# Attention followed by a soft mixture of experts: slot sums from the accumulated D^T P, grouped narrow products, and an output in larger chunks

## The chip, the cores and the metric

The kernel runs on one core of one Trainium2 chip. The metric is the device time of one execution in microseconds (us). The engines are called as the profile calls them: PE (TensorE; PEld is its weight load), DVE (VectorE), ACT (ScalarE), POOL (GpSimd) and SP (SyncE, which here only issues DMAs).

## The reference, cut to what matters

```python
kv_pool = kv.reshape(B, H//4, 4, W//4, 4, C).mean(axis=(2, 4))
k = v = kv_pool.reshape(B, -1, C) @ w_sr               # 768 keys per batch, C = 128
a = softmax((q @ k.T) / sqrt(C), -1);  x = (a @ v).reshape(B * S, D)   # B = 4, S = 12288 queries
logits = x @ phi                                       # 49152 tokens x 32 slots
d = exp(logits - logits.max(0)); d /= d.sum(0) + 1e-9  # softmax over the tokens
slot_input = d.T @ x                                   # 32 x 128
slot_out = per expert e (8, of 4 slots): relu(slot_input @ w1[e]) @ w2[e]   # hidden 1024
c = exp(logits - logits.max(1)); c /= c.sum(1) + 1e-9  # softmax over the slots
out = c @ slot_out                                     # 49152 x 128
```

Inputs and output are float32. `q` is given to the kernel transposed, and the output is written transposed (`outT`, 128 x 49152).

## The kernel before

The kernel never forms x. With P the unnormalised attention weights of a tile, logits are (P U)/rowsum with U = v phi (768 x 32), and the slot input is (D^T P) v.

**A tile** is 128 queries; there are 384, 96 in each batch. `qk` (L348) makes scores in one of three score slots in PSUM (`sslot`, tag "s", two banks each) from high and low parts of q and k, six matmuls. `top` (L358) finds the row maximum on DVE, `exp` (L365) makes P in float32 on ACT with its row sum, `hi` and `lo` (L377 on ACT, L381 on POOL) split the first 512 of 768 keys into two float16 halves, and `turn` (L384) turns these by DMA transposes issued on SP. The last 256 keys are turned in PE for two tiles at a time (`tp`, L389) and copied out by DVE (`tev`, L396).

**A group** is eight tiles; the last eight form two groups of four, which makes 49 groups. `lmm` (L405) makes its logits, transposed, in the bank "L": `lmm(g, 0)` from the float32 part, then three more steps from the float16 parts. Their weights are 32 columns wide and four of them share the PE array side by side. `lt_out`, `lt_turn`, `recip`, `logits` scale and turn them back into `LL`, which keeps the logits of all tokens. `colmax`, `cross`, `newmax` update the running column maximum, `weights` makes e = exp(logits - max) on ACT, and `scaled` divides by the row sums, which gives D. `total_mm` (L516) sums e over the tokens by matmuls against a vector of ones, and `total` (L525) adds this to the running sum `EA`, faded by `decay` when the maximum has moved. `ymm` (L532) makes D^T P of two tiles, in four steps y0, y2, y4, y6, in the bank "D"; its weights too are 32 columns wide. `yacc` adds it to `acc`. `rowmax`, `rowsub` (POOL), `rowexp` turn `LL` into the unnormalised c.

**A batch** begins with its keys (loaded by SP, added up by POOL in eight steps during the batch before: `kv_load`, `kv_add`, `kv_fold`) and ends with `yturn` and `slots`, which multiply acc with v and add to the slot input `SA`.

**The bank D** is shared: the turned tiles of `tp`, D^T P and the key products use it one after the other (ring "D" of one). The bank L has a ring of one as well.

**The order on every engine** is made ahead by a planner (`Plan`, L26): each operation has an engine, a cost, a latency, dependencies, buffers that it takes and a priority; the planner runs through time and always lets an engine take the operation of smallest priority among those that can start within 0.12 us of the first one. `LATE` shifts the priorities by kind of operation.

**The tail** first loads the expert weights (4 MB each of w1 and w2) into buffers that the tiles leave, then runs the experts (`t_sm` to `t_slo`). `k_sum`, `k_add`, `k_rec`, `k_mul` (L882 to L897) make the row sums of c for 16 tiles at a time, add eps, take the reciprocal and multiply (POOL). The output goes by chunks of CH = 3 quads (a quad is four tiles): `c_t` turns c in PE, `c_hi` and `c_lo` split it, `o_mm` (L916) multiplies it with the slot outputs, 32 rows at a time, into two score slots, `o_ev` copies one on DVE and the other on ACT into one buffer, and `o_dma` (L936) writes it. The first two chunks are written by halves (two of each four tiles), all others whole.

Of the kernel before, what the change touches and what calls it, by code (L numbers as in the profile page):

```python
# [19 lines left out]
P = 128  # L20
# [5 lines left out]
class Plan:  # L26
# [3 lines left out]
    HOLD = 0.7  # L30
# [6 lines left out]
    def op(self, eng, cost, lat, prio, deps, fn, acq=(), use=(), at=0.0, raw=0.1, hot=False):  # L37
        n = len(self.ops)
        for key in list(acq) + list(use):
            self.users.setdefault(key, []).append(n)  # L40
        self.ops.append((eng, cost, lat, prio, [d for d in deps if d is not None], fn, list(acq), at, raw, hot, list(use)))
        return n

    def emit(self):
# [18 lines left out]
        free = dict.fromkeys(avail, 0.0)  # L63
        todo = len(ops)
# [10 lines left out]
        def best(e):  # L75
            found = []
            for n in avail[e]:
                t = acquire(n)
                if t is not None:
                    found.append((max(free[e], ready[n], t), ops[n][3], n))  # L80
            if not found:
                return None
            t0 = min(found)[0] + 0.12
            hot = [f for f in found if ops[f[2]][9]]
            if hot:
                h = min(hot)
                if h[0] - t0 < self.HOLD:
                    fits = [(p, t, n) for t, p, n in found if t <= t0 and t + ops[n][1] <= h[0] + 0.1]
                    return min(fits) if fits else (h[1], h[0], h[2])
            return min((p, t, n) for t, p, n in found if t <= t0)  # L90

        self.starts = [None] * len(ops)
        while todo:
# [7 lines left out]
            self.starts[n] = t  # L101
            free[e] = t + cost
# [20 lines left out]
def attention_then_soft_moe(ctx: ExitStack, tc: tile.TileContext, qT, kv0, kvT, w_sr, w_srT, phi, w1, w2, outT):  # L123
# [59 lines left out]
    eps = cp.tile([P, 1], F32, tag="eps", name="eps")  # L183
    nc.vector.memset(eps, EPS)
# [14 lines left out]
    EA = cp.tile([P, 1], F32, tag="EA", name="EA")  # L199
    MB = cp.tile([P, NS], F32, tag="MB", name="MB")  # L200
# [204 lines left out]
    def lmm(g, n):  # L405
# [3 lines left out]
        if n == 0:  # L409
            G[g] = {"L": bank("L", f"L_{g}")}  # L410
# [105 lines left out]
    def total_mm(g):  # L516
        G[g]["D"] = bank("D", f"D_{g}")
        n = groups[g][1] // NQD
        for x in range(n):
            nc.tensor.matmul(  # L520
                G[g]["D"][:, NT * NS : NT * NS + 1], G[g]["e"][:, x * NQD : (x + 1) * NQD, :], ones[:, :1],
                start=(x == 0), stop=(x == n - 1),
            )

    def total(g):  # L525
        t = G[g]["D"][:, NT * NS : NT * NS + 1]
        if g:
            nc.vector.scalar_tensor_tensor(out=EA, in0=EA, scalar=G[g]["al"], in1=t, op0=ALU.mult, op1=ALU.add)
# [29 lines left out]
    def rowexp(g):  # L558
        nc.scalar.activation(ll(g), ll(g), AF.Exp, scale=-1.0)

# [34 lines left out]
    def pool(n):  # L595
# [85 lines left out]
    def group_ops(g):  # L681
# [4 lines left out]
        lk = ("L", g)  # L686
# [15 lines left out]
        l0 = (0.52 if n == GMAX else 0.3, 0.2)  # L702
        l1 = (0.44 if n == GMAX else 0.3, 0.2)
        a = go("l0", "PE", l0, [ops["tev", u] for u in us] + [ops["u", b]], lambda: lmm(g, 0), acq=[lk], use=pfs + [("U", b)])
        for x in range(3):
            a = go(f"l{x + 1}", "PE", l1, [a] + (turns if x == 0 else []), lambda x=x: lmm(g, x + 1), use=[lk, ("U", b)] + pts, raw=0.0)
# [5 lines left out]
        a = go("cx", "PE", (0.24, 0.25), [a], lambda: cross(g), use=[lk])  # L712
# [4 lines left out]
        al = go("al", "ACT", (0.19, 0.1), [a], lambda: decay(g)) if g else None  # L717
        d = go("dp", "DVE", dv(0.33), [w, rc], lambda: scaled(g), acq=[("dp", g)], use=[lk, ("e", g)])
        y = t = go("tm", "PE", (0.22 * n / GMAX, 0.25), [w], lambda: total_mm(g), acq=[("D", g)], use=[("e", g)])
        for t0 in range(0, n, 2):  # L720
            y = go(f"y{t0}", "PE", (0.67, 0.2), [y, d], lambda t0=t0: ymm(g, t0, t0 + 2), use=[("dp", g), p32[t0 // 2], ("D", g)], raw=0.0)
        ya = go("ya", "DVE", (0.42, 0.08), [y, al, ops.get(("yt", b - 1)) if first else ops["ya", g - 1]], lambda: yacc(g), use=[("D", g)])
        go("to", "DVE", (0.13, 0.08), [y, al, ops.get(("to", g - 1))], lambda: total(g), use=[("D", g)])
        rm = go("rm", "DVE", dv(0.33), [sb], lambda: rowmax(g))
        rm = go("rs", "POOL", dv(0.57, 0.02), [rm], lambda: rowsub(g))
        ops["c", g] = go("re", "ACT", dv(0.31, 0.1), [rm], lambda: rowexp(g))
        if (s + n) % TPB == 0:
# [3 lines left out]
            ops["sl", b] = sl  # L731
            m = go("ms", "DVE", (0.35, 0.1), [ops["nm", g], ops.get(("sa", b - 1))], lambda: mstep(b, g), use=[lk])
# [5 lines left out]
    for i in range(NTL):  # L738
        b = i // TPB
        t = T(i)  # L740
        iq = i // TB
        if i % TB == 0:
            if iq >= 1 and iq + 2 < NB:
                ops["q", iq + 2] = op("SP", 0.75, 2.0, t - 2, [ops["ql", iq - 1], ops["q", iq + 1]], lambda n=iq + 2: q_load(n), acq=[("q", iq + 2)])
            for n in ([0, 1] if iq == 0 else [iq + 1]):
                if n < NB:
                    a = op("ACT", 0.54, 0.1, t + LATE["qh"] if n else -50, [ops["q", n], ops.get(("ql", n - 1))], lambda n=n: q_hi(n), acq=[("qs", n)], use=[("q", n)])
                    ops["ql", n] = op("POOL", 1.24, 0.02, t + LATE["ql"] if n else -50, [a], lambda n=n: q_lo(n), use=[("qs", n), ("q", n)])
        kd = [ops["k", b, 0], ops["k", b, 1]]
        ops["qk", i] = op("PE", 1.03, 0.24, t + LATE["qk"], [ops["ql", iq], ops.get(("qk", i - 1))] + kd, lambda i=i: qk(i), acq=[("s", i)], use=[("qs", iq), ("kT", b)], raw=0.0)  # L750
        a = op("DVE", 0.92, 0.06, t + LATE["top"], [ops["qk", i]], lambda i=i: top(i), use=[("s", i)])
        ops["e", i] = op("ACT", 0.89, 0.1, t + LATE["exp"], [a, ops.get(("e", i - 1))], lambda i=i: exp(i), acq=[("p32", i // 2)] if i % 2 == 0 else [],
                         use=[("s", i)] + ([("p32", i // 2)] if i % 2 else []), raw=0.0)
        a = ops["hi", i] = op("ACT", 0.53, 0.1, t + LATE["hi"], [ops["e", i], ops.get(("hi", i - 1))], lambda i=i: hi(i), acq=[("hl", i)], use=[("p32", i // 2)], raw=0.15)
        a = op("POOL", 1.12, 0.02, t + LATE["lo"], [a], lambda i=i: lo(i), use=[("hl", i), ("p32", i // 2)])
        ops["turn", i] = op("SP", 1.45, 2.2, t + 6, [a, ops.get(("turn", i - 1))], lambda i=i: turn(i), acq=[("pt", i // 2)] if i % 2 == 0 else [],
                            use=[("hl", i)] + ([("pt", i // 2)] if i % 2 else []))
        if i % 2:
            u = i // 2
            dk = ("D", ("t", u))  # L760
            a = op("PE", 0.38, 0.24, t + LATE["tp"], [ops["e", i]], lambda u=u: tp(u), acq=[dk], use=[("p32", u)], raw=0.0)
            ops["tev", u] = op("DVE", 0.6, 0.06, t + LATE["tev"], [a, ops.get(("tev", u - 1))], lambda u=u: tev(u), acq=[("pf", u)], use=[dk])
# [20 lines left out]
    CH = 3  # L783
# [98 lines left out]
    def k_sum(x):  # L882
        o, n = kg[x]
        nc.vector.tensor_reduce(out=RM[:, o : o + n], in_=LL[:, o : o + n, :], axis=X, op=ALU.add)

    def k_add(x):
        o, n = kg[x]
        nc.scalar.activation(RM[:, o : o + n], RM[:, o : o + n], AF.Identity, bias=eps)

    def k_rec(x):  # L890
        o, n = kg[x]
        nc.vector.reciprocal(out=RM[:, o : o + n], in_=RM[:, o : o + n])  # L892

# [12 lines left out]
    def c_hi(g):  # L906
        n = chunks[g][1] * P
        UC[g, "c"] = ring("pt", [P, 2, HK], F32R, f"c_{g}")
# [18 lines left out]
    def o_ev(g, u):  # L927
        n = chunks[g][1] * P
        src = UC[g, "po", u][:, :, :n].rearrange("p t (j q) -> p t j q", q=P)
        dst = UC[g, "o"][:, :, 2 * u : 2 * u + 2, :].rearrange("p j t q -> p t j q")  # L930
# [5 lines left out]
    def o_dma(g, t0, t1):  # L936
        o, n = chunks[g]
        nc.sync.dma_start(
            out=outT[:, o * TS * P : (o + n) * TS * P].rearrange("p (j t q) -> p j t q", t=TS, q=P)[:, :, t0:t1, :],
            in_=UC[g, "o"][:, :, t0:t1, :],  # L940
# [21 lines left out]
    a = tail("PE", 0.3, [ops["to", LAST]], t_es, acq=[("L", "pe")])  # L962
# [27 lines left out]
    for x, (o, n) in enumerate(kg):  # L990
        w = n * NS
        p = T1 + 288 + 4 * x
        need = [ops["c", GOF[o]], ops["c", GOF[o + n - 1]]]
        a = op("DVE", dve(w), 0.08, p, need + [qt if x < 6 else slo], lambda x=x: k_sum(x))
        a = op("ACT", 0.18, 0.08, p, [a], lambda x=x: k_add(x))
# [60 lines left out]
```

## Time and profile before

| what | us |
|---|---|
| runs | 987.91, 987.96, 994.11; median 987.96 |
| the profiled execution's own time | 990.42 |
| its span | 988.6 |
| mean granted PE clock in it | 0.956 |
| busy: PE, DVE, ACT, POOL | 916.7, 758.2, 745.2, 693.3 |

The page says how long each engine was busy, how the 40 slices of the span look, and which groups of instructions cost most. Answers of the trace show single instructions in order of time (start and length in us from the span's start), the busy time of each engine in a stretch, and the chain of waits that ended last. "L537" is line 537 of the kernel before. The planner repeats the same order for many groups, so one group read instruction by instruction says much about the loop. fp32 matmuls are recorded as two instructions.

### The profile page before, as it was taken

What the parts mean: (1) busy time and instruction counts of PE and PEld (TensorE: products, weight loads), DVE (VectorE), ACT (ScalarE), POOL (GpSimd) and SP (SyncE); (2) the same over time, 40 slices, a digit from 0 to 9 for tenths busy, and PEclk for the clock granted to TensorE, in tenths of its full rate; (3) what the DMA queues carried; (4) which work ended last, traced back from release to release, by engine and by line L of the source; (5) the groups of instructions that cost most, each with busy time, mean ns of one, the idle gap of its engine ahead of it and who ended that gap; (6) DMA issues with size and microseconds to landing.
All of it is one profiled execution on the core that took longest, in us unless ns stands there. A gap on an engine that the chain in (4) does not pass through costs nothing.

```text
span 988.6 us, 27483 instructions
## 1 busy us (share of the span) xinstructions
PE 916.7 (93%) x10392; PEld 773.8 (78%) x10392; DVE 758.2 (77%) x1894; ACT 745.2 (75%) x1571; POOL 693.3 (70%) x584
## 2 busy tenths in 40 slices
PE   0999999999999999999999999999999999968875
PEld 0878988888888888888888888888798989844543
DVE  6667888788768787877778788788687888846775
ACT  1688888888868887878868888888688888813554
POOL 2498999876779988876789989767577777612222
PEclk9999999999999999999999999999999999987566
DMA  7499999897889999987999999988698898992877
GB/s 303 91 233 181 203 210 212 156 161 139 157 212 199 205 189 182 163 152 151 163 226 204 189 204 171 170 139 153 127 155 162 155 163 149 127 349 75 337 302 324
DMA packets 433011, 186.49 MB, mean 189 GB/s; under 512 B 408560, under 2 KB 410352, under 8 KB 432880
## 3 DMA queue, kind: packets, MB, share of 16 engines
q1 hardware_dynamic: 432304, 184.35, 87.9%
q8 instruction: 81, 1.33, 0.5%
q10 hardware_dynamic: 576, 0.41, 0.1%
q14 instruction: 50, 0.41, 0.1%
HBM read 58.87 MB, written 25.17 MB: 85 GB/s over the span
## 4 chain that ended last, share of the span: by engine, by line
PE 47%; DVE 4%; ACT 3%; issue 1%; DMA 0%; DVEq 0%; ACTq 0%; SPq 0%
PE s L356 20%; PE DB L537 8%; PE L L414 6%; PE DB L394 4%; PE po L925 3%; DVE o L934 1%; PE DB L520 1%; PE L L439 1%; ACT hl L379 1%; DVE junk L360 1%; ACT p L372 1%; ACT o L932 1%; PE ph L826 1%; PE DB L904 1%; DVE pf L398 0%
## 5 line engine op out<-in xcount | busy, mean ns | idle before, releaser
L382 POOL TENSOR_TENSOR hl<-p,hl 128x512 f16<-128x512 f32 x384 | 442.2, 1167 | 144.1 <-ACT hl L379 128.2
L356 PE MATMUL s<-kT,qs 128*128 128x384 f32 x2304 | 479.5, 350 | 2.3 <-ACT p L372 2.3
L360 DVE CUSTOM_DVE_ANT_1 junk<-s,lnpk 128x768 bf16<-128x768 f32 x384 | 366.2, 954 | 70.8 <-PE s L356 52.5
L356 PEld LDWEIGHTS s<-kT,qs 128*128 128x128 f32 x2304 | 392.4, 190 | 25.1 <-issue 19.1
L372 ACT ACTIVATE p<-s,nm 128x768 f32<-128x768 f32 x384 | 344.7, 899 | 89.1 <-PE DB L537 41.7
L379 ACT ACTIVATE hl<-p 128x512 f16<-128x512 f32 x384 | 235.2, 625 | 5.5 <-DMA pt<-hl 0.7
L346 POOL TENSOR_TENSOR qs<-q,qs 128x512 fp32r<-128x512 f32 x96 | 125.2, 1304 | 45.9 <-ACT qs L343 27.9
L398 DVE COPY pf<-DB 128x512 f32<-128x512 f32 x192 | 131.8, 686 | 19.4 <-PE DB L394 12.8
L537 PE MATMUL DB<-p,dp 128*32 128x192 f32 x3072 | 146.7, 332 | 0.0
L394 PE MATMUL DB<-ident,p 128*128 128x128 f32 x768 | 118.4, 276 | 12.1 <-DVE pf L398 9.1
L537 PEld LDWEIGHTS DB<-p,dp 128*32 128x32 f32 x3072 | 90.5, 110 | 29.2 <-issue 9.2
L394 PEld LDWEIGHTS DB<-ident,p 128*128 128x128 f32 x768 | 95.0, 141 | 22.0 <-DVE pf L398 10.2
L255 POOL TENSOR_TENSOR LL<-LL 128x1536 f32<-128x1536 f32 x21 | 73.3, 3491 | 2.6 <-DMA LL<-kvT 2.3
L372 ACT ACTIVATION_READ_ACCUMULATOR p<-s,nm 128x1 f32 x384 | 74.7, 195 | 0.0
L414 PE MATMUL L<-pt,u 128*32 128x256 f16 (+1 forms) x2352 | 73.5, 272 | 0.0
L897 POOL TENSOR_TENSOR LL<-LL,RM 128x512 f32<-128x512 f32 x24 | 24.9, 1048 | 67.1 <-DVE RM L892 67.1
L414 PEld LDWEIGHTS <-u 128*32 128x32 f16 x2352 | 63.9, 98 | 10.0 <-issue 1.9
L343 ACT ACTIVATE qs<-q 128x512 fp32r<-128x512 f32 x96 | 59.8, 623 | 11.8 <-DMA q<-qT 9.6
L414 PE MATMUL L<-pf,us 128*32 128x256 f32 (+1 forms) x784 | 54.1, 394 | 0.0
L925 PE MATMUL po<-c,shl 32*128 32x384 f32 x384 | 40.4, 502 | 13.8 <-DVE o L934 11.2
L435 ACT ACTIVATE lt<-L,g 128x256 f32<-128x256 f32 (+1 forms) x49 | 23.0, 469 | 38.7 <-PE L L414 38.7
L932 ACT ACTIVATE o<-po 128x768 f32<-128x768 f32 x32 | 25.9, 810 | 29.0 <-PE po L925 29.0
(132 smaller groups left out, 745.2 us busy)
## 6 DMA issues: line engine op xcount, KB each, us to landing
q<-qT SPq DMA_DIRECT2D x95, 256.0 KB, 3.2
outT<-o SPq DMA_DIRECT2D x30, 768.0 KB, 3.6
LL<-kvT SPq DMA_DIRECT2D x24, 768.0 KB, 5.1
kv<-kv SPq DMA_DIRECT2D x8, 768.0 KB, 9.1
pt<-hl SPq DMA_TRANSPOSE x384, 3.3
w<-w SPq DMA_DIRECT2D x7, 768.0 KB, 7.3
w<-w SPq DMA_DIRECT2D x11, 256.0 KB, 7.7
outT<-o SPq DMA_DIRECT2D x4, 384.0 KB, 3.0
```

Source lines behind the costliest of these rows:

```text
L255: nc.gpsimd.tensor_tensor(out=stage[:, 2:4, :], in0=stage[:, 2:4, :], in1=stage[:, 0:2, :], op=ALU.add)
L346: nc.gpsimd.tensor_tensor(out=QSP[i][:, 1], in0=QS[i], in1=QSP[i][:, 0].bitcast(F32), op=ALU.subtract)
L356: nc.tensor.matmul(s[:, h, :HK], a, k[:, m, h * HK : (h + 1) * HK], start=(n == 0), stop=(n == 2))
L360: nc.vector.tensor_tensor_reduce(out=junk.rearrange("p (h k) -> p h k", h=2), in0=S[i][:, :, :HK], in1=lnpk.unsqueeze(2).broadcast_to([P, ...
L372: nc.scalar.activation(P32[i // 2][:, i % 2, :].rearrange("p (h k) -> p h k", h=2), S.pop(i)[:, :, :HK], AF.Exp, bias=NM.pop(i), scale=1.0 ...
L379: nc.scalar.activation(HL[i][:, 0], P32[i // 2][:, i % 2, : KD * P], AF.Copy)
L382: nc.gpsimd.tensor_tensor(out=HL[i][:, 1], in0=P32[i // 2][:, i % 2, : KD * P], in1=HL[i][:, 0], op=ALU.subtract)
L394: nc.tensor.transpose(out=DB[:, o : o + P], in_=P32[u][:, h, k * P : (k + 1) * P], identity=ident)
L398: nc.vector.tensor_copy(PF[u].rearrange("p x h q -> p (x h q)"), DB[:, : 2 * KP * P])
L414: nc.tensor.matmul(out.rearrange("p (h q) -> p h q", q=P) if gt(g) == 2 else out, lhs, rhs, start=start, stop=stop)
L537: nc.tensor.matmul(G[g]["D"][j * NS : (j + 1) * NS, : NT * NS].rearrange("p (k r) -> p k r", k=NT), G[g]["dp"][:, t, :], p[:, j], start=(t ...
L925: nc.tensor.matmul(UC[g, "po", t // 2][:, t % 2, : n * P], s[rows, a, :C], c[rows, m, : n * P], start=(k == 0), stop=(k == 2))
```

## The change

1. **Slot sums.** `total_mm` and its matmuls with ones are gone. A row sum of D^T P is the sum of e (up to eps), so once a batch `total` sums `acc` over its 768 entries and adds this to `EA`, faded by `be` = exp(old max - new max) (`fade`, ACT).
2. **The planner** drops its rule on "hot" operations and knows a mode for each: narrow products (l0 to l3, y0 to y6) have mode 1, and PE's cost rises by 0.12 when it goes from 0 to 1 and by 0.22 from 1 to 0. Priorities have new values, for tile operations one for each place in the group.
3. **The last group** takes score slots for its L and its D instead of the two banks.
4. **Sums of c in the loop.** `rownorm` (DVE: reduce, add eps, reciprocal) follows each group's `rowexp`; `k_sum`, `k_add`, `k_rec` are gone from the tail, and `k_mul` waits for the groups alone.
5. **The output** goes by chunks of CH = 4 quads; each half has a buffer of its own and is written by itself.

```diff
-    def op(self, eng, cost, lat, prio, deps, fn, acq=(), use=(), at=0.0, raw=0.1, hot=False):
+    SWITCH = {(0, 1): 0.12, (1, 0): 0.22}
+    def op(self, eng, cost, lat, prio, deps, fn, acq=(), use=(), at=0.0, raw=0.1, mode=0):
...
+            cost += self.SWITCH.get((last.get(e, 0), ops[n][9]), 0.0)
+            last[e] = ops[n][9]
...
-            G[g] = {"L": bank("L", f"L_{g}")}
+            G[g] = {"L": sslot(f"L_{g}")[:, 0, :] if g == LAST else bank("L", f"L_{g}")}
...
-    def total_mm(g):
-        G[g]["D"] = bank("D", f"D_{g}")
-        n = groups[g][1] // NQD
-        for x in range(n):
-            nc.tensor.matmul(
-                G[g]["D"][:, NT * NS : NT * NS + 1], G[g]["e"][:, x * NQD : (x + 1) * NQD, :], ones[:, :1],
-                start=(x == 0), stop=(x == n - 1),
-            )
-
-    def total(g):
-        t = G[g]["D"][:, NT * NS : NT * NS + 1]
-        if g:
-            nc.vector.scalar_tensor_tensor(out=EA, in0=EA, scalar=G[g]["al"], in1=t, op0=ALU.mult, op1=ALU.add)
+    def total(b, g):
+        es = G[g]["es"] = wp.tile([P, 1], F32, tag="es", name=f"es_{b}", bufs=1)
+        nc.vector.tensor_reduce(out=es, in_=acc, axis=XY, op=ALU.add)
+        if b:
+            nc.vector.scalar_tensor_tensor(out=EA, in0=EA, scalar=be, in1=es, op0=ALU.mult, op1=ALU.add)
         else:
-            nc.vector.tensor_copy(EA, t)
+            nc.vector.tensor_copy(EA, es)
+        nc.vector.tensor_copy(CB, G[g]["c"])
+
+    def fade(b, g):
+        nc.scalar.activation(be, G[g]["c"], AF.Exp, bias=CB, scale=-1.0)
 
     def ymm(g, t0, t1):
         s, n = groups[g]
+        if t0 == 0:
+            G[g]["D"] = sslot(f"D_{g}")[:, 0, :] if g == LAST else DB
...
+    def rownorm(g):
+        s, n = groups[g]
+        r = RM[:, s : s + n]
+        nc.vector.tensor_reduce(out=r, in_=ll(g), axis=X, op=ALU.add)
+        nc.vector.tensor_scalar_add(r, r, EPS)
+        nc.vector.reciprocal(out=r, in_=r)
...
-        y = t = go("tm", "PE", (0.22 * n / GMAX, 0.25), [w], lambda: total_mm(g), acq=[("D", g)], use=[("e", g)])
+        y = None
...
-    CH = 3
+    CH = 4
...
-        UC[g, "o"] = ring("p32", [P, 2, NK], F32, f"o_{g}").rearrange("p a b -> p (a b)")[:, : n * TS * P].rearrange("p (j t q) -> p j t q", t=TS, q=P)
         for u in range(2):
+            UC[g, "o", u] = ring("p32", [P, 2, NK], F32, f"o_{g}_{u}").rearrange("p a b -> p (a b)")[:, : 2 * n * P].rearrange("p (j t q) -> p j t q", t=2, q=P)
             UC[g, "po", u] = sslot(f"po_{g}_{u}")
...
-    def o_dma(g, t0, t1):
+    def o_dma(g, u):
         o, n = chunks[g]
         nc.sync.dma_start(
-            out=outT[:, o * TS * P : (o + n) * TS * P].rearrange("p (j t q) -> p j t q", t=TS, q=P)[:, :, t0:t1, :],
-            in_=UC[g, "o"][:, :, t0:t1, :],
+            out=outT[:, o * TS * P : (o + n) * TS * P].rearrange("p (j t q) -> p j t q", t=TS, q=P)[:, :, 2 * u : 2 * u + 2, :],
+            in_=UC[g, "o", u],
         )
```

More of the change, by code (lines that the diff above doesn't have):

```diff
@@ L40, in op @@
             self.users.setdefault(key, []).append(n)
-        self.ops.append((eng, cost, lat, prio, [d for d in deps if d is not None], fn, list(acq), at, raw, hot, list(use)))
+        self.ops.append((eng, cost, lat, prio, [d for d in deps if d is not None], fn, list(acq), at, raw, mode, list(use)))
         return n
@@ L63, in emit @@
         free = dict.fromkeys(avail, 0.0)
+        last = {}
         todo = len(ops)
@@ L731, in group_ops @@
             ops["sl", b] = sl
+            fd = go("fd", "ACT", (0.19, 0.1), [ops["nm", g], ops["to", b - 1]], lambda: fade(b, g)) if b else None
+            ops["to", b] = go("to", "DVE", (0.75, 0.1), [ya, fd], lambda: total(b, g))
             m = go("ms", "DVE", (0.35, 0.1), [ops["nm", g], ops.get(("sa", b - 1))], lambda: mstep(b, g), use=[lk])
@@ L741, in attention_then_soft_moe @@
         iq = i // TB
+        x = i - groups[GOF[i]][0]
         if i % TB == 0:
@@ L746, in attention_then_soft_moe @@
                 if n < NB:
-                    a = op("ACT", 0.54, 0.1, t + LATE["qh"] if n else -50, [ops["q", n], ops.get(("ql", n - 1))], lambda n=n: q_hi(n), acq=[("qs", n)], use=[("q", n)])
-                    ops["ql", n] = op("POOL", 1.24, 0.02, t + LATE["ql"] if n else -50, [a], lambda n=n: q_lo(n), use=[("qs", n), ("q", n)])
+                    a = op("ACT", 0.54, 0.1, t + LATE["qh"][(4 * n - groups[GOF[4 * n]][0]) // 4] if n else -50, [ops["q", n], ops.get(("ql", n - 1))], lambda n=n: q_hi(n), acq=[("qs", n)], use=[("q", n)])
@@ L749, in attention_then_soft_moe @@
+                    ops["ql", n] = op("POOL", 1.24, 0.02, t + LATE["ql"][(4 * n - groups[GOF[4 * n]][0]) // 4] if n else -50, [a], lambda n=n: q_lo(n), use=[("qs", n), ("q", n)])
         kd = [ops["k", b, 0], ops["k", b, 1]]
-        ops["qk", i] = op("PE", 1.03, 0.24, t + LATE["qk"], [ops["ql", iq], ops.get(("qk", i - 1))] + kd, lambda i=i: qk(i), acq=[("s", i)], use=[("qs", iq), ("kT", b)], raw=0.0)
-        a = op("DVE", 0.92, 0.06, t + LATE["top"], [ops["qk", i]], lambda i=i: top(i), use=[("s", i)])
@@ L757, in attention_then_soft_moe @@
+        a = op("POOL", 1.12, 0.02, t + LATE["lo"][x], [a], lambda i=i: lo(i), use=[("hl", i), ("p32", i // 2)])
+        ops["turn", i] = op("SP", 1.45, 2.2, t + LATE["turn"][x], [a, ops.get(("turn", i - 1))], lambda i=i: turn(i), acq=[("pt", i // 2)] if i % 2 == 0 else [],
                             use=[("hl", i)] + ([("pt", i // 2)] if i % 2 else []))
@@ L880, in attention_then_soft_moe @@
     kg = [(o, 2 * GMAX) for o in range(0, NTL, 2 * GMAX)]
[L882 to L892, printed above, removed]
     def k_mul(x):
@@ L992, in attention_then_soft_moe @@
         p = T1 + 288 + 4 * x
-        need = [ops["c", GOF[o]], ops["c", GOF[o + n - 1]]]
-        a = op("DVE", dve(w), 0.08, p, need + [qt if x < 6 else slo], lambda x=x: k_sum(x))
-        a = op("ACT", 0.18, 0.08, p, [a], lambda x=x: k_add(x))
-        a = op("DVE", 0.2, 0.08, p, [a], lambda x=x: k_rec(x))
-        KC[x] = op("POOL", 1.05 * w / 512, 0.1, p, [a, qt if x < 4 else sq[1]], lambda x=x: k_mul(x))
+        need = [ops["c", g] for g in range(GOF[o], GOF[o + n - 1] + 1)]
+        KC[x] = op("POOL", 1.05 * w / 512, 0.1, p, need + [ops["turn", NTL - 1]], lambda x=x: k_mul(x))
     for g, (o, n) in enumerate(chunks):
```

85 lines of the change are left out of this document (42 added, 43 removed), and 9 rows, old and new, of the table LATE.

## The prediction

> **What bounds the kernel now.** I read the page's busy times first, then the busy times by stretch, then the order of time on TensorE (PE).
>
> ```profile
> PE 916.7 (93%) x10392; PEld 773.8 (78%) x10392; DVE 758.2 (77%) x1894; ACT 745.2 (75%) x1571; POOL 693.3 (70%) x584
> ```
>
> The average says PE. It mixes the loop over the 384 tiles with what follows it, so the next view takes stretches of 17 us, one in the loop with a load of the next batch's keys and one without. Columns: PE, PE's weight loads, DVE, ACT, POOL (busy us, instructions), granted clock, DMA share, GB/s.
>
> ```profile
> 538.00:555.00 17.00, 17.00 (x204) 14.84 (x203) 13.54 (x36) 14.69 (x31) 15.89 (x14) 1.00 1.09 208
> ...
> 776.00:793.00 17.00, 17.00 (x224) 14.94 (x216) 14.07 (x36) 14.58 (x31) 12.63 (x13) 1.00 0.86 159
> ```
>
> In both PE never stops, at full clock. DVE and ACT have over 2 us of 17 free; POOL has 4.4 us free in the second stretch and only 1.1 in the first, where it also adds up the next keys. Now what PE does in one group of eight tiles (start, modelled length, line, what, records; I use the distance from one start to the next, because the lengths overlap):
>
> ```profile
> 763.01 2.16 PE L537 MATMUL DB<-p,dp 128*32 128x192 f32 x48
> ...
> 774.10 0.60 PE L394 MATMUL DB<-ident,p 128*128 128x128 f32 x4
> 774.62 1.07 PE L414 MATMUL L<-pf,us 128*32 128x256 f32 x16
> 775.51 1.49 PE L414 MATMUL L<-pt,u 128*32 128x256 f16 x48
> 776.94 1.31 PE L356 MATMUL s<-kT,qs 128*128 128x384 f32 x6
> 778.09 0.50 PE L520 MATMUL DB<-ones,e 128*128 128x1 f32 x4
> 778.52 0.86 PE L537 MATMUL DB<-p,dp 128*32 128x192 f32 x16
> 779.31 0.44 PE L439 MATMUL L<-ident,lt 128*128 128x128 f32 x2
> 779.67 2.16 PE L537 MATMUL DB<-p,dp 128*32 128x192 f32 x48
> 781.76 1.34 PE L356 MATMUL s<-kT,qs 128*128 128x384 f32 x6
> ```
>
> One group lasts 779.67 - 763.01 = **16.66 us**, all of it PE work in order. Three stretches use weights 32 columns wide (128*32): L (774.62 to 776.94), the first quarter of D^T P (778.52 to 779.31), and its rest (779.67 to 781.76). Between them stand products of full width.
>
> **The loop, part by part.** The stretches allow a fit. D^T P takes 0.79 us for 16 records and 2.09 us for 48: 0.0406 us a record, and 0.14 us on leaving the narrow form. That the 0.14 belongs to the change of width, another group shows, where narrow L follows narrow D^T P:
>
> ```profile
> 565.82 0.86 PE L537 MATMUL DB<-p,dp 128*32 128x192 f32 x16
> 566.50 1.06 PE L414 MATMUL L<-pt,u 128*32 128x256 f16 x32
> 567.48 1.32 PE L356 MATMUL s<-kT,qs 128*128 128x384 f32 x6
> ...
> 601.07 0.38 PE L439 MATMUL L<-ident,lt 128*128 128x128 f32 x2
> 601.21 1.32 PE L356 MATMUL s<-kT,qs 128*128 128x384 f32 x6
> ```
>
> There the same 16 records take 0.68 us. For L: 48 records in 1.43 us, 32 in 0.98, so 0.028 a record and 0.08 on leaving. And the two transposes of L (L439) take 0.36 us ahead of narrow products but 0.14 us between wide ones: 0.22 us for entering. With L and D^T P in one block, the ones products gone and the transposes after the block, a group loses:
> - the ones products (L520): 778.52 - 778.09 = 0.43;
> - leaving L for a score product: 0.08;
> - leaving the first quarter of D^T P: 0.14;
> - entering its rest behind the transposes: 0.22.
>
> Sum 0.87 us, so 16.66 becomes 15.79. The first entry and the last exit stay. 46 groups stand in the loop (49 less the last three): 46 x 0.87 = **-40.0 us**, as long as PE stays the bound.
>
> Does it? Per group (a row above times 16.66/17) ACT has 14.58 -> 14.29 us of work, 90% of 15.79. DVE has 13.79 and gains the sums of c, which are one reduce of 128x256, an add and a reciprocal on eight columns, and it loses one small update of EA:
>
> ```profile
> L552 DVE TENSOR_REDUCE rm<-LL 128x8 f32<-128x256 f32 x47 | 19.4, 413 | 0.0
> ...
> L528 DVE SCALAR_TENSOR_TENSOR EA<-EA,al,DB 128x1 f32<-128x1 f32 x48 | 9.9, 205 | 0.0
> ```
>
> The reduce is of L552's shape (0.41), the two small ones I take at L528's 0.2 each; 0.81 - 0.21 = +0.6, so 14.4 us, 91%. They hang on nothing that waits in the loop, since RM is read in the tail only; what could be queued behind them on DVE is the search for a tile's maximum, for at most 0.8 us, and three score slots cover that. Four times in all EA is built from acc (a reduce of 192, under 0.41, an update, a copy): 4 x 0.8 us of DVE, beside PE work, at nothing; without cover it would be 3 us. The fade of EA is one small ACT operation a batch.
>
> POOL is the tight one. With the keys' adds it has 15.89 x 16.66/17 = 15.57 us of work in a group of 15.79, and it works in order, waiting now and then for ACT. By the code some 24 groups are of this kind (seven adds and a fold in each of three batches). Bounds: 0, if it keeps up, and 24 x 0.87 = 21, if it holds these groups at 16.66. Its work fits, so I stay near the lower end: 0.2 us a group, **+5 us**. SP only issues, and the DMA share of 1.09 lies beside a PE without a wait; the same transfers in 5% less time I cost at nothing.
>
> **The drain behind the loop.** The last two groups have four tiles each and share one bank for L and one for D:
>
> ```profile
> 870.69 0.66 PE L394 MATMUL DB<-ident,p 128*128 128x128 f32 x4
> ...
> 877.57 0.86 PE L537 MATMUL DB<-p,dp 128*32 128x192 f32 x16
> 878.24 0.62 PE L414 MATMUL L<-pf,us 128*32 128x128 f32 x16
> ...
> 885.07 2.79 PE L537 MATMUL DB<-p,dp 128*32 128x192 f32 x32
> ```
>
> The copy that follows a turn is this group of the page:
>
> ```profile
> L398 DVE COPY pf<-DB 128x512 f32<-128x512 f32 x192 | 131.8, 686 | 19.4 <-PE DB L394 12.8
> ```
>
> The last tiles are turned at 870.69, and with 0.66 and a copy out of 0.69 group 48's L could start at 872.1. It starts at 878.24, after group 47 has used its bank. In a score slot of its own it can start 6 us earlier; its chain to the end of D^T P (878.24 to 887.86, 9.6 us) then runs beside group 47's on DVE, for which I give back 1.5, and it loses its ones products (0.5). **-5 us**, bounds 0 (if the order of maxima holds it) and -7. What is late next: the expert weights, two 4 MB loads that the score chain used to hide; they start as tiles' slots come free and so move up with it.
>
> **The output.** All 34 writes stand in one row of the write queue:
>
> ```profile
> 909.36 75.03 SPq L938 DMA_DIRECT2D outT<-o  x34
> ```
>
> From the first issue to the span's end are 79.2 us, for 32 chunks of three quads. Two rates are seen; the first two chunks are written by halves, in runs of 1 KB, all others in runs of 6 KB:
>
> ```profile
> 913.00:914.00 1.00, 0.43 (x4) 0.43 (x8) 0.98 (x2) 0.67 (x1) 0.00 (x0) 0.50 1.00 341
> ...
> 919.00:920.00 1.00, 0.38 (x6) 0.00 (x0) 0.89 (x2) 0.81 (x1) 0.00 (x0) 0.50 1.03 430
> ```
>
> After the change every write is a half with runs of 1 KB (two of four tiles of 128 values). At 341 GB/s the 25.17 MB take 73.8 us, and DMA is full all the while. The engines' cycle of a chunk now, without the sums of c in it:
>
> ```profile
> 913.57 1.04 PE po L925 x6
> 914.64 0.97 DVE o L934
> 915.61 0.04 issue
> 915.65 1.33 PE po L925 x9
> ```
>
> The next chunk's products wait for DVE's copy of the last one: 1.07 us of products and 0.97 of copy, 2.08 with the hand-overs. With four quads, both by 4/3, about 2.7 us, and 24 x 2.7 = 65 us. The sums, eps and reciprocals of c leave the tail, and POOL's products are done before it. So DMA becomes the bound: 73.8 + 0.6 for the larger first chunk + 2 for the start and the last landing = 76.4 against 79.2: **-3 us**, bounds +3 (writes wait for engines in turn) and -11 (engines bound, 65 + 3).
> [...]
>
> **Sum.** -40.0 + 5 - 5 - 3 = -43 us. The profiled execution took 990.42 us (span 988.6): 947.4. The median shown, 987.96, lies 2.5 below it: **945 us**.
>
> **Rivals.**
> - POOL holds the groups with key adds at 16.66. For: 15.57 of 15.79 us busy and every lower half waits for ACT in order. Against: six buffers of halves and six of turned pairs lie between it and PE. Only 22 groups then gain: 22 x 0.87 = 19; 990.4 - 19 - 8 - 2.5 = 961. Chance 0.16.
> - The change doesn't do what it says: the planner leaves score products between L and D^T P, so one more exit (0.08) and entry (about 0.2) stay: 46 x 0.28 = 13 us less gain, 958. For: the order comes of priorities, and in parts of the run before it differs from group to group. 0.10.
> - Runs of 1 KB go at the full rate once many are under way: 8 us more gain, 937. For: only about 4 us of such writes are seen. Against: DMA share was 1.00 in them. 0.10.
> - Slower: the block starves ACT. It lasts 0.89 + 1.35 + 2.74 = 4.98 us without a new score. ACT has 14.29/8 = 1.79 us of work a tile, so with n filled slots at its start it idles 4.98 - 1.79 n, and the period becomes 14.29 + 4.98 - 1.79 n. With three slots filled it is covered; with n under 1.46 a group is longer than 16.66; at n = 1 it is 17.5: 46 x 0.82 = +38, less 8, less 2.5: 1018. Speaking for it: DVE, busier than before, fills slots' maxima late. 0.08. At n near 1.5 the loop gains nothing, and only the tail's 8 us stay: 980, which is within 1%. 0.06.
>
> **How the numbers follow.** My forecast, 937 to 953 by the bounds of POOL, drain and output, has 0.50. The range leaves out the last two cases (0.14) and the ends: 929 (full-rate writes, a POOL that costs nothing, and some of the stalls where batches meet recovered) to 966 (POOL, with an output at +3). A measurement of this kernel tells a difference of about 1%, 10 us, from none. Faster by more: 0.50 + 0.16 + 0.10 + 0.10 = 0.86; within: 0.06; slower: 0.08.
>
> **What would show it.** In PE's order of time: L and D^T P back to back, some 5.0 us, and a period of 15.8 us. If the period is right in groups without key adds and 16.2 or more with them, POOL's term was the wrong one. If ACT's waits for PE grow over 2 us a group, it is the block. In the drain, L of the last group should start within 2 us of the last turn; in the output, DMA share at 1.0 and 340 GB/s throughout. The prediction fails most if the block starves the engines that PE feeds, or if the rows of one period don't stand for the loop.

## The result and the profile after

The changed kernel takes 981.41 us (median of 20 runs, 971.14 to 994.51) against 988.72 for the kernel before in the same series (984.72 to 994.11): a ratio of 0.9894, 95% interval 0.9871 to 0.9918. The ratio is of fast runs alone: six of the 20 (987.44 us and more) are marked slow, and the other 14 have a median of 979.65 us. Forecast were 945 us and a range from 929 to 966: the kernel gained about 1% where 4% were expected. The profiled execution took 979.63 us, its span 977.8, at a mean granted clock of 0.960. (Of the lines from here on, those of after and its variants carry numbers of their own code: D^T P is L532, the score products L353, the transposes of L are L436.)

The page's busy times of after show the first odd thing, PE and DVE:

```profile
PE 872.0 (89%) x10104; PEld 742.7 (76%) x10104; DVE 798.4 (82%) x1939; ACT 727.4 (74%) x1531; POOL 688.8 (70%) x584
```

PE has 45 us less to do than before (916.7), in line with the fewer turns of width and the ones products gone. But the span shrank by only 10.8, and DVE has 40 us **more** (758.2 before), where the sums of c were counted at 0.6 us a group, 29 in all, and the tail's own sums go (L884 and L892 of before, 15.4 and 5.6 us). The two stretches that were shown of before, in the same columns:

```profile
538.00:555.00 17.00, 16.74 (x201) 14.97 (x202) 14.77 (x40) 14.43 (x32) 17.00 (x14) 1.00 1.09 204
776.00:793.00 17.00, 16.81 (x203) 14.92 (x203) 14.96 (x39) 14.88 (x32) 12.40 (x12) 1.00 0.92 166
```

PE now pauses in both. POOL, in the stretch with key adds, is full (17.00 where it had 15.89). PE's order of time in one group:

```profile
563.85 1.33 PE L353 MATMUL s<-kT,qs 128*128 128x384 f32 x6 [0.19 <-ACT p L369]
565.10 1.07 PE L411 MATMUL L<-pf,us 128*32 128x256 f32 x16
565.99 1.49 PE L411 MATMUL L<-pt,u 128*32 128x256 f16 x48
567.30 2.78 PE L532 MATMUL DB<-p,dp 128*32 128x192 f32 x64
570.01 0.44 PE L436 MATMUL L<-ident,lt 128*128 128x128 f32 x2
570.21 1.29 PE L353 MATMUL s<-kT,qs 128*128 128x384 f32 x6
...
578.48 1.30 PE L353 MATMUL s<-kT,qs 128*128 128x384 f32 x6
579.97 1.32 PE L353 MATMUL s<-kT,qs 128*128 128x384 f32 x6 [0.19 <-ACT p L369]
581.22 1.07 PE L411 MATMUL L<-pf,us 128*32 128x256 f32 x16
```

The change does what it says: L and D^T P stand in one block of 570.01 - 565.10 = 4.91 us, the transposes behind it. The group lasts 581.22 - 565.10 = 16.12 us (16.66 before, 15.79 forecast). The bracket is a wait: ahead of the last score product of each quiet group PE stands idle for a score slot until `exp` frees it. ACT itself is idle twice in this group, 0.27 us at 567.60 and 1.60 us behind the block:

```profile
572.72 0.90 ACT L369 ACTIVATE p<-s,nm 128x768 f32<-128x768 f32 x1 [1.60 <-DVE nm L357]
```

From there on it has no idle time over 0.15 us until the next block begins.

Such groups are not the whole loop. From the first start of L (group 0) to the last of a full group (46) are 46 periods; the two rows of each, before first:

```profile
48.84 1.36 PE L414 MATMUL L<-pf,us 128*32 128x256 f32 x16
...
857.92 1.07 PE L414 MATMUL L<-pf,us 128*32 128x256 f32 x16
```

```profile
49.84 1.07 PE L411 MATMUL L<-pf,us 128*32 128x256 f32 x16
...
849.55 1.07 PE L411 MATMUL L<-pf,us 128*32 128x256 f32 x16 [0.60 <-DVE dp L511]
```

That is 809.08 us before and 799.71 after: -9.4 where 46 x (16.66 - 16.12) would give -24.8. Before, 46 quiet periods leave 42.7 us for longer groups (the ends of batches above all); after, 58.2. Two groups of after in the middle of a batch last 22.5 and 24.25 us. In the second of them (PE's L at 351.13 and 375.38) lies this, from the order of time on all engines:

```profile
350.85 4.54 POOL L379 TENSOR_TENSOR hl<-p,hl 128x512 f16<-128x512 f32 x4
...
353.56 7.58 DVE L560 TENSOR_SCALAR RM<-RM 128x8 f32<-128x8 f32 x1
...
355.35 1.27 POOL L343 TENSOR_TENSOR qs<-q,qs 128x512 fp32r<-128x512 f32 x1
...
356.58 3.42 POOL L252 TENSOR_TENSOR LL<-LL 128x1536 f32<-128x1536 f32 x1
...
359.95 1.16 POOL L379 TENSOR_TENSOR hl<-p,hl 128x512 f16<-128x512 f32 x1
...
362.04 0.66 PE L436 MATMUL L<-ident,lt 128*128 128x128 f32 x2 [5.93 <-DVE L L506]
...
365.66 0.90 ACT L369 ACTIVATE p<-s,nm 128x768 f32<-128x768 f32 x1 [8.21 <-DVE nm L357]
```

L560 is the add of eps in `rownorm`, to **eight columns**. It stays on DVE for 7.58 us. POOL works without a gap from 350.85 to 361.11, and at 361.14 the add ends. Behind it on DVE stand the small steps of L (L506), for which PE waits 5.93 us, and the next maximum (`top`, L357), for which ACT waits 8.21. The groups of instructions of after put it beside the same operation (another add of eps) with its output in PSUM:

```profile
L560 DVE TENSOR_SCALAR RM<-RM 128x8 f32<-128x8 f32 (+1 forms) x49 | 45.6, 930 | 1.7
...
L444 DVE TENSOR_SCALAR L<-sums 128x8 f32<-128x8 f32 (+1 forms) x49 | 8.1, 166 | 17.0 <-ACT lt L432 16.0
```

Most of the 49 adds wait less. A usual one, with the instructions of POOL around it:

```profile
631.30 1.28 POOL L343 TENSOR_TENSOR qs<-q,qs 128x512 fp32r<-128x512 f32 x1 [0.80 <-ACT qs L340]
631.59 1.01 DVE L560 TENSOR_SCALAR RM<-RM 128x8 f32<-128x8 f32 x1
632.54 1.15 POOL L379 TENSOR_TENSOR hl<-p,hl 128x512 f16<-128x512 f32 x1
```

It ends at 632.60, 0.02 us after the instruction of POOL that ran when it started, although POOL's next one is already at work. Taken one by one, 46 of the 49 last over 190 ns. In 44 of them the add ends some 0.03 us after that one instruction of POOL; the two others, of 5.48 us (at 125.94) and 7.58 us, run over five, the first of them with POOL still at work behind it. Why these two were not served at the first end **stays open**.

With the long ones the granted clock of PE falls as well. PE stops for 3.76 us (to 132.32) and 5.93 us (to 362.04) behind these two, and from 131.09 and from 359.79 on the clock stands at 0.50 for 6.83 us each; the first score product in it (132.63 and 362.35) takes 2.27 us both times, against 1.29 at 570.21, where the clock is 1.00.

The forecast gave the add 0.2 us and no effect. The theory to test, called the port theory in the expectations (the name is the author's; no run shows a port): this add waits for POOL, and DVE with all that is queued on it waits too. The rivals: the gain is lost to POOL's own lateness in groups with key adds (the forecast's rival), or the block's waits for a slot are all of it, and the add only fills idle time.

### The profile page after: what moved, and what is told of

It reads as the page before. It is cut to its first block, busy times and chain, and to the rows that moved or that the text cites. A ratio compares the mean times of both kernels' runs of the same rounds, so it can differ in the third digit from the quotient of the medians.

```text
span 977.8 us, 26937 instructions
## 1 busy us (share of the span) xinstructions
PE 872.0 (89%) x10104; PEld 742.7 (76%) x10104; DVE 798.4 (82%) x1939; ACT 727.4 (74%) x1531; POOL 688.8 (70%) x584
## 3 DMA queue, kind: packets, MB, share of 16 engines
q8 instruction: 79, 1.29, 0.6%
## 5 line engine op out<-in xcount | busy, mean ns | idle before, releaser
L353 PE MATMUL s<-kT,qs 128*128 128x384 f32 x2304 | 487.7, 352 | 6.8 <-ACT p L369 6.2
L353 PEld LDWEIGHTS s<-kT,qs 128*128 128x128 f32 x2304 | 393.0, 191 | 22.2 <-ACT p L369 18.4
L357 DVE CUSTOM_DVE_ANT_1 junk<-s,lnpk 128x768 bf16<-128x768 f32 x384 | 364.9, 950 | 26.3 <-PE s L353 10.5
L376 ACT ACTIVATE hl<-p 128x512 f16<-128x512 f32 x384 | 231.1, 626 | 7.2 <-DMA pt<-hl 3.7
L532 PE MATMUL DB<-p,dp 128*32 128x192 f32 x3040 | 135.1, 328 | 4.2 <-DVE pf L395 3.5
L532 PEld LDWEIGHTS DB<-p,dp 128*32 128x32 f32 x3040 | 96.8, 110 | 30.1 <-DVE pf L395 8.4
L542 DVE SCALAR_TENSOR_TENSOR acc<-acc,al,DB 128x192 f32<-128x192 f32 x44 | 18.1, 412 | 44.8 <-PE DB L532 44.8
L411 PE MATMUL L<-pf,us 128*32 128x256 f32 (+1 forms) x784 | 51.5, 380 | 2.2 <-DVE dp L511 2.0
L929 PE MATMUL po<-c,shl 32*128 32x512 f32 x288 | 37.1, 554 | 11.2 <-ACT o L936 7.5
L560 DVE TENSOR_SCALAR RM<-RM 128x8 f32<-128x8 f32 (+1 forms) x49 | 45.6, 930 | 1.7
L938 DVE COPY o<-po 128x1024 f32<-128x1024 f32 x24 | 29.3, 1221 | 19.5 <-DMA outT<-o 12.2
```

Of the source, the lines that this page charges most:

```text
L353: nc.tensor.matmul(s[:, h, :HK], a, k[:, m, h * HK : (h + 1) * HK], start=(n == 0), stop=(n == 2))
L357: nc.vector.tensor_tensor_reduce(out=junk.rearrange("p (h k) -> p h k", h=2), in0=S[i][:, :, :HK], in1=lnpk.unsqueeze(2).broadcast_to([P, ...
L376: nc.scalar.activation(HL[i][:, 0], P32[i // 2][:, i % 2, : KD * P], AF.Copy)
L411: nc.tensor.matmul(out.rearrange("p (h q) -> p h q", q=P) if gt(g) == 2 else out, lhs, rhs, start=start, stop=stop)
L532: nc.tensor.matmul(G[g]["D"][j * NS : (j + 1) * NS, : NT * NS].rearrange("p (k r) -> p k r", k=NT), G[g]["dp"][:, t, :], p[:, j], start=(t ...
```

## The experiments

**The add as a reduce** (eps_reduce). Each group's sum is written beside a constant eps, and a second reduce over the pair takes the place of the add; as many DVE instructions, in the same places.

```diff
-        nc.vector.tensor_reduce(out=r, in_=ll(g), axis=X, op=ALU.add)
-        nc.vector.tensor_scalar_add(r, r, EPS)
+        nc.vector.tensor_reduce(out=RM2[:, :n, 0], in_=ll(g), axis=X, op=ALU.add)
+        nc.vector.tensor_reduce(out=r, in_=RM2[:, :n, :], axis=X, op=ALU.add)   # RM2[:, :, 1] = EPS
         nc.vector.reciprocal(out=r, in_=r)
```

> The changed kernel with one instruction per group in another form: eps is added to the row sums of c by a reduce over pairs (sum, eps) instead of by a tensor_scalar; the order on every engine and the number of instructions are the same. Port theory (the tensor_scalar on SBUF alone waits while POOL works, 930 ns on average and up to 7.6 us, and holds up the row maxima behind it): the instruction takes about 0.17 us, DVE is about 36 us less busy, the group period between key loads goes from 16.1 to 15.8 us, and the time falls from 981 us by 15 to 30 us, to 951 to 966. Block theory (five microseconds of narrow products starve ACT, and DVE has room enough): the instruction gets shorter, the time stays within 5 us of 981. POOL theory (groups with key adds are held by POOL itself): at most 8 us gained.

Measured: 955.27 us (6 runs, 951.57 to 958.87), ratio to before 0.9646 (0.9613 to 0.9679). One instruction of eight columns, in another form, is worth 24 us against the 979.65 of after. In the trace of eps_reduce the summary of the line (smallest, median and largest duration in ns), the page's busy times, and first L, last full L and first output product:

```profile
L562 DVE TENSOR_REDUCE RM<-RM x49: 161/170/172, 73.5 to 850.8; 128x8 f32<-128x16 f32 x47, 128x4 f32<-128x8 f32 x2
```

```profile
PE 863.2 (91%) x10104; PEld 738.6 (78%) x10104; DVE 758.9 (80%) x1940; ACT 727.7 (77%) x1531; POOL 690.2 (73%) x584
```

```profile
50.12 1.07 PE L413 MATMUL L<-pf,us 128*32 128x256 f32 x16
...
825.30 1.07 PE L413 MATMUL L<-pf,us 128*32 128x256 f32 x16 [0.59 <-DVE dp L513]
...
870.32 2.08 PE L931 MATMUL po<-c,shl 32*128 32x512 f32 x14 [0.46 <-ACT shl L891]
```

The loop is 775.18 us, 33.9 shorter than before's; the forecast had -40 + 5. (This profile is of the fastest of the six runs, and the profiled run of before is 1.7 us above its median; the medians of this series, 990.88 for before, differ by 35.6 us, the spans by 38.8.) Quiet groups last 16.12 to 16.15 as in after, not the 15.8 expected; what went are the long ones. Compared group by group, after's loop is 24.5 us longer, and 20.0 of these lie in four groups, those whose adds took 7.58, 5.48, 3.10 and 3.08 us; the other 42 make 4.5 us together. In eps_reduce the granted clock stays at 1.00 through the whole loop; no score product that stands alone in PE's order of time takes over 1.36 us in it. DVE is back by 39.5 us at one instruction more than after.

**No eps at all** (no_eps). The line `tensor_scalar_add(r, r, EPS)` is deleted; the eps of 1e-9 is missing in c.

> The changed kernel without the add of eps to the row sums of c (a row sum is at least 1, and 1 + 1e-9 is 1 in float32); 49 DVE instructions fewer, the order otherwise the same. Port theory: as with the add as a reduce, 951 to 966 us, and within 4 us of it, since 49 x 0.17 us of DVE work is all that differs. Block theory and POOL theory: 973 to 984.

957.73 us (952.39 to 960.57), 0.9669 (0.9634 to 0.9704): the same as eps_reduce. So the reduce that stands in for the add costs nothing that can be measured, and the loss is the add's form, not the third instruction. Nor is it that the data lie in SBUF: the reciprocal behind the add, on the same eight columns, never waits. Its summary in after:

```profile
L561 DVE RECIPROCAL RM<-RM x49: 178/203/206, 74.4 to 875.7; 128x8 f32<-128x8 f32 x47, 128x4 f32<-128x4 f32 x2
```

**The add in the kernel before** (before_port, before_port2). If the add is so dear, it should harm before as well. It is put on eight columns of scratch that nobody reads, at two places:

```diff
+    scr = cp.tile([P, GMAX], F32, tag="scr", name="scr")
 def yacc(g):                      # before_port; in before_port2 behind the reduce in rowmax
+        nc.vector.tensor_scalar_add(scr, scr, EPS)
```

> The kernel before with one tensor_scalar on eight columns of a scratch tile in SBUF added per group, in front of the update of acc; its result is not used, and the order is otherwise the same. Port theory: it lasts 0.5 us or more on average, several us at the worst, and the kernel gets slower by 5 to 25 us (993 to 1013). If only the instruction's own 0.17 us counted (DVE is 77% busy and PE is the bound): within 3 us of 988.

> The kernel before with the same unused tensor_scalar on eight columns in SBUF, now behind the row maxima of a group's logits (DVE), where the trace of before has POOL at work: in groups without key adds for about 4 us on end (757.0 to 761.1), in groups with them for 0.4 to 0.7 us. Port theory: the instruction lasts until POOL pauses, 1 to 4 us on average, and the kernel takes 995 to 1040 us. If it is the instruction and not POOL that costs: 0.17 us and no change, as at its first place.

before_port: 991.77 us, ratio 1.0012 (0.9991 to 1.0034), no change, and a miss. before_port2: 1002.65 us in the median of four runs, ratio 1.0104 (1.0066 to 1.0143), slower by 1%; a fifth run took 1764.50 us, for which nothing here gives a cause, and is not in these figures. The line's summaries (smallest, median, largest), before_port first:

```profile
L545 DVE TENSOR_SCALAR scr<-scr x49: 159/164/906, 80.0 to 884.7; 128x8 f32<-128x8 f32 x49
```

```profile
L555 DVE TENSOR_SCALAR scr<-scr x49: 160/278/2598, 64.8 to 898.8; 128x8 f32<-128x8 f32 x49
```

At the first place POOL is idle when the add starts in 23 of 49 cases (one falls at 764.46, in a POOL gap from 764.13 to 765.21), and the add takes 390 ns on the mean; at the second place in 13, and it takes 651. The instruction and its operands are the same, so it is the moment that sets its price. Every wait here ends with the instruction of POOL that was running at the start, so the waits are shorter than the 1 to 4 us a time that I expected.

**POOL unloaded** (after_fewadds, fix_fewadds). That POOL is what the add waits for was so far read from one stretch. So its largest instructions, the 21 key adds of 3.5 us, are cut to their first eight columns, in after and in eps_reduce (keys of batches 1 to 3 are left unsummed):

```diff
-        nc.gpsimd.tensor_tensor(out=stage[:, 2:4, :], in0=stage[:, 2:4, :], in1=stage[:, 0:2, :], op=ALU.add)
+        nc.gpsimd.tensor_tensor(out=stage[:, 2:4, :8], in0=stage[:, 2:4, :8], in1=stage[:, 0:2, :8], op=ALU.add)
```

> The kernel after, with the 21 key adds on POOL (3.5 us each) cut to their first 8 columns, so that the keys of batches 1 to 3 are not the reference's; all else as it is. Theory: the add of eps to eight columns (mean 930 ns, 45.6 us in all, longest 7.58 us) waits until POOL pauses, and POOL runs back to back in the groups with key adds. Then its longest falls under 4 us, its total to 10 to 25 us, and the kernel takes 945 to 960 us. Rival: the add is slow by itself or because of something other than POOL's load; its mean stays at 800 ns or more, and the time falls by less than 10 us.

> eps_reduce with the same cut of the key adds: what is POOL's load still worth when the add of eps is gone? Theory (POOL-late lower halves make the transposes late, and PE stalls in the block): the groups of 18 to 19.5 us go, the loop ends 8 to 20 us earlier than eps_reduce's (its last eight-tile D^T P block starts at 827.5), time 937 to 948. Rival: the load is covered; within 4 us of eps_reduce.

after_fewadds: 961.79 us (959.34 to 964.62), 0.9703 (0.9677 to 0.9729). The untouched add gets shorter because another engine has less to do; its summary in after, then in after_fewadds:

```profile
L560 DVE TENSOR_SCALAR RM<-RM x49: 169/598/7581, 73.2 to 874.9; 128x8 f32<-128x8 f32 x47, 128x4 f32<-128x4 f32 x2
```

```profile
L560 DVE TENSOR_SCALAR RM<-RM x49: 170/332/1295, 73.5 to 861.8; 128x8 f32<-128x8 f32 x47, 128x4 f32<-128x4 f32 x2
```

The longest falls from 7.58 to 1.30 us, the total from 45.6 to 27.2 (49 x 554 ns, a little above what I expected), and the loop from 799.71 to 784.35 us (L at 50.13 and 834.48). No add runs over a second instruction of POOL any more, and the order of the instructions in the loop is the same as in after.

fix_fewadds: 954.34 us (953.01 to 957.58), 0.9632 (0.9606 to 0.9659), the same as eps_reduce: the theory of late lower halves predicted 937 to 948 and fell. **The same cut of POOL's work is worth some 18 us with the add in place (979.65 to 961.79), and nothing that can be measured without it (955.27 to 954.34).** The load of the key adds does not hold the loop; it holds the add. The 9 us of loop that still separate after_fewadds (784.35) from eps_reduce (775.18) are probably the waits that remain, 554 ns on the mean; no run takes these apart.

**The sums back in the tail** (sums_tail). `rownorm` is left empty, and reduce, eps and reciprocal of c stand in the tail again, eps on ACT, as before.

> The changed kernel without any sums of c in the loop (the three DVE instructions a group are left out, the order is otherwise the same); they are made in the tail as in the kernel before. Port theory, with the add as the whole cost: the loop is as fast as with the add as a reduce (start of the last eight-tile D^T P at 825 to 830 us of the span, 852.7 with the tensor_scalar). If the two other instructions matter as well: before 822. The tail gets longer by 2 to 10 us.

966.03 us (963.91 to 966.45), 0.9746 (0.9716 to 0.9776): slower than eps_reduce, with a loop of 791.34 us, 16 longer than eps_reduce's, which I had expected it to match or beat. The tail, which was to get 2 to 10 us longer, is 1.0 shorter from the last full L on. Three single groups (22.75, 22.95 and 21.98 us) make up most of the 16. In the second, PE stops inside L:

```profile
367.38 2.74 PE L413 MATMUL L<-pt,u 128*32 128x256 f16 x45 [5.04 <-DMA pt<-hl]
```

Here a DMA transpose is late, not DVE: six of them, issued from 356.98 on behind a load of keys (356.35), take 12.5 us on the queue. The two other stops are 3.73 and 4.10 us, and behind all three the granted clock falls to 0.50 for a while (6.83, 3.41 and 3.41 us); D^T P behind them takes 4.35, 3.27 and 3.20 us, against 2.78 at 567.30 in after. eps_reduce stops in the same way in two groups, for 1.94 and 2.53 us, and keeps its clock (D^T P behind both takes 2.87 us); best has one long group of this kind (22.56 us from 87.8 on). after and all its variants keep one order of instructions on PE, DVE, ACT, POOL and SP in the loop, so why these stops differ so much **stays open**. A loop can thus differ by some 16 us for a reason other than the add; what ties the 24.5 us between after and eps_reduce to the add is the comparison by groups above and the cut of the key adds.

**The output** (out3). After with CH = 3 and whole writes, as before.

```diff
-    CH = 4
+    CH = 3
-        dst = UC[g, "o", u].rearrange("p j t q -> p t j q")     # a buffer and a write for each half
+        dst = UC[g, "o"][:, :, 2 * u : 2 * u + 2, :].rearrange("p j t q -> p t j q")   # one write in runs of 6 KB
```

> The changed kernel with the output of the kernel before: chunks of three quads, whole writes in runs of 6 KB (the first two chunks by halves); the sums of c stay in the loop. Theory that runs of 1 KB bound the output at 341 GB/s: from the first output product to the end 79.1 us become 68 to 72 (engines' cycle of about 2.1 us x 32, 61 us of writes at 416 GB/s), the time falls by 7 to 11 us, to 970 to 974. If the engines bound the output all the same: 79 us stay, 981 within 3.

974.74 us (969.93 to 983.56), 0.9846 (0.9803 to 0.9889). From the first output product to the end are 68.3 us, against 79.1 in after (898.70 to 977.8). A stretch of the output, with the columns of the stretches above, in after and then in out3:

```profile
920.00:930.00 10.00, 8.91 (x87) 5.52 (x80) 9.76 (x13) 8.03 (x13) 0.00 (x0) 1.00 1.03 339
```

```profile
940.00:950.00 10.00, 9.33 (x90) 5.44 (x82) 8.30 (x12) 6.60 (x11) 0.00 (x0) 1.00 1.02 415
```

DMA is full in both; writes in runs of 1 KB move 339 GB/s, those in runs of 6 KB 415. The writes differ in size as well (512 KB and 768 KB); the halves of 384 KB in before moved 341 GB/s in runs of 1 KB, which speaks for the run, but no run here changes it alone. The profiled run of out3 has 13 us more loop than that of after, with the same instructions in the same order. 12.9 of the 13 lie in two groups, in which the add took 7.57 us (0.70 in after) and 9.96 (5.48 in after): with the add in it, the same loop lasts longer or shorter by how often an add runs over several instructions of POOL.

**Late products, and the best of all** (reduce_late, best, fix_out3). The products of c on POOL now start early, among the last groups. reduce_late is eps_reduce with `k_mul` put behind the slot input in the planner's order; best is reduce_late with the output of out3; fix_out3 is eps_reduce with the output of out3 alone.

```diff
-        KC[x] = op("POOL", 1.05 * w / 512, 0.1, p, need + [ops["turn", NTL - 1]], lambda x=x: k_mul(x))
+        KC[x] = op("POOL", 1.05 * w / 512, 0.1, p, need + [s1], lambda x=x: k_mul(x))
```

> The changed kernel with eps added by a reduce, and POOL's products of c held back until the slot inputs are copied for the experts, so that POOL rests in the drain and no output transposes take the bank D ahead of the last D^T P. Theory that this early output work held the drain (two copies of 0.17 us took 2.1, the last D^T P and the slot product waited for parts of c): from the end of D^T P of group 46 to the first output product 36 us or less instead of 40.1, time 950 to 953 against 955.3. If the drain is its own chain: 40 us, no change; if the output then lacks its c: over 957.

> As reduce_late, and the output by chunks of three quads in runs of 6 KB. If the gains add: 955.3 less 4 for the drain less 8 to 10 for the output, 941 to 944 (before: 988 to 991). If the chunks of three need their c earlier than POOL gives them: over 948.

> eps_reduce with before's output (chunks of three quads, whole writes in runs of 6 KB), c multiplied as early as in eps_reduce. Theory: the output takes 67 to 69 us as in out3 and best, with eps_reduce's loop: 943 to 946, the same as best or 2 us below it. Rival: POOL's early products of c delay the last groups, 947 to 950.

reduce_late: 956.37 us, 0.9647 (0.962 to 0.9675), the same as eps_reduce; from the last full group's D^T P to the first output product both take 40.07 us, so starting the products later gains nothing. The edit did not make POOL rest as it was meant to: the products start at 850.86, ahead of the two copies at 857.13, which still take 0.84 and 1.09 us beside them, so what an idle POOL would give in the drain is not shown. best: **945.86 us** (942.84 to 949.22), 0.9547 (0.9519 to 0.9574), 2 us above its forecast, as the drain's gain did not come. fix_out3: 947.54 us (940.51 to 949.37), 0.9544 (0.9509 to 0.9579), not to be told from best. With the add in another form and before's output, the change comes to the time that was forecast for it; as the sum behind it is another, that is luck.

## Why the prediction was wrong, step by step

The step that failed is the cost of the sums of c: "the two small ones I take at L528's 0.2 each", and "they hang on nothing that waits in the loop". The add hangs on POOL. It measured 0.93 us on the mean and 7.58 at most, and the cover of three score slots, counted for 0.8 us, ends long before that; in place of nothing it cost 24.5 us of loop in the profiled runs (21.2 against no_eps), 20.0 of them in the four groups with its longest waits. The price came from a row of another operation (L528 reads PSUM), and nearly all small DVE work in the loop of before touches PSUM, where no such wait is seen (L528 took at most 212 ns, an add of eps with its output in PSUM, L447, 173), so a mean of before could not show it. The change moved that very update into SBUF as well (L517 of after): three instructions with a mean of 954 ns in place of 205, which were priced at nothing. One line of before might have hinted at it, with four instructions, a subtraction within SBUF (smallest, median, largest):

```profile
L318 DVE SCALAR_TENSOR_TENSOR u<-uf,inv,u x4: 343/344/1069, 36.2 to 654.6; 128x128 f16<-128x128 f32 x4
```

The runs tell the forms apart: the reduce in the add's place took at most 172 ns in eps_reduce, and the form that waits is the add within SBUF. In after 44 of its 46 waits end with one instruction of POOL; the two that ran over five, and three such in out3, go beyond that. What makes one form wait and the other not is not shown.

- **Loop, -40.0 from 0.87 a group.** The parts are there: one block of 4.91 us, 45 us less PE work. With the add gone the loop is -33.9, near the forecast net of -35, but partly for another reason. The period is 16.13, not 15.79: eight score products at the usual distance of 1.13 us (574.24 to 575.37 is one) would take 9.04 us and take 9.44, and 0.36 of it lies between 578.48 and 579.97, where PE waits for ACT. The step that failed here is "as long as PE stays the bound". In the group shown, ACT's work of 14.01 us, its idle time of 1.87 us and gaps of under 0.15 us fill the 16.12, so ACT bounds the period. That is the rival "the block starves ACT" at a small size, though below the sign of 2 us that was set for it. 46 x 0.53 = 24.4; the other 9.5 come from longer groups that got shorter (42.7 to 33.2 us beyond 46 quiet periods), which no step of mine had, so that -33.9 lies near -35 is partly luck. At least some of the 9.5 is clock: before stands at 0.50 three times for 3.41 us in its loop (from 68.34, 283.38 and 706.63 on; the score product at 283.73 takes 2.27 us), eps_reduce never.
- **POOL, +5.** With the add removed, it is within what can be measured of 0 (eps_reduce against fix_fewadds). The rival "POOL holds the groups with key adds" was wrong in its way: the key adds act through the add on DVE (three of its four longest waits lie beside one), not through POOL's own lateness, and a group with POOL at work for 16.06 of 16.12 us (565.10 to 581.22) is as short as the others.
- **Drain, -5.** L of the last group starts at 861.99, 2.1 us after the last turn (859.88), about as said, but its D^T P still ends after group 47's: from the end of the last full D^T P to the first output product are 43.35 us before, 43.28 after, 40.07 in eps_reduce. So nothing came of the 5 us with the add. Without it the drain takes 42.95 us in no_eps, 42.65 in fix_fewadds, 44.65 in fix_out3 and 39.54 in best, so the 3 us of eps_reduce are not a sure gain either. Whether the order of maxima holds it, my bound of 0, is not shown.
- **Output, -3.** Right: 79.1 us against 81.2, from the first output product, DMA full at 339 GB/s. The row's rate held for 48 writes, and whole writes in runs of 6 KB, at 415 GB/s in out3, save another 11 us (68.3 against 79.1).

The sum of spans closes: start +1.0, loop -9.4, last block (from the last full L to the end of its D^T P) -0.2, drain -0.1, output -2.1 give the -10.8 of after; in eps_reduce +1.3, -33.9, -1.2, -3.3 and -1.8 give the -38.8 but for rounding.

## What to carry to other kernels

Price a small DVE instruction by its form and by who else is at work, not by its size: where POOL is busy most of the time (70% of the span in after), a tiny add within SBUF waited for up to 7.58 us in after and 9.96 in out3, and everything queued behind it on DVE waited with it. Look at the largest duration of a line beside its mean: here the largest was twelve times the median, and a few long waits did most of the harm (20.0 of 24.5 us in four groups). The wait shows as busy time of DVE (45.6 us for the 49 adds of after), not as idle time. A reduce over a pair with a constant did the same work here without the wait (at most 172 ns), and an add of eps whose output lies in PSUM had none (at most 171 ns).

## What the runs showed of the hardware

- An add of a constant to 128x8 float32 within SBUF took 159 to 172 ns beside an idle POOL (after, before_port, before_port2). Beside a busy one it mostly ended some 0.03 us after the instruction of POOL that ran at its start (44 of 46 waits in after, all in before_port and before_port2); in after two, and in out3 three, ran over five to seven instructions, up to 9.96 us. The same add with its output in PSUM stayed within 171 ns in after and 173 in before, a reduce of 128x16 within 172, a reciprocal of 128x8 within SBUF within 206.
- Other forms with all operands in SBUF were longer beside a busy POOL: the split of U (L318 of before) took 343 to 344 ns three times with POOL idle and 1069 once with POOL at work; the copy of the slot input (16 columns) took 168 and 175 ns in before, with POOL idle, and 1.07 us on the mean in after (L826), beside POOL's products.
- With stops of PE of 3.76 and 5.93 us in the loop of after the granted clock fell to 0.50 for 6.83 us each. In before it did so for 3.41 us behind stops of 1.56, 2.18 and 2.19 us, but not behind another of 2.18 us (to 495.45), so the length of a stop alone does not tell.
- Writes in runs of 1 KB held 339 to 342 GB/s in after with 48 writes in a row; those in runs of 6 KB held 411 to 415 in the middle of the outputs of out3, best and fix_out3, at a DMA share over 1.0 in all of them.
